# A planned attention and GLU kernel: the third score tile's PSUM banks go to transposes at batch 1's first score tile, and batch 1 counts 35 tiles behind

## The chip, the core and the metric

The kernel runs on one core of a Trainium2 chip. The metric is the device time of one execution in microseconds (us); lower is better. The core has a matrix engine (PE, with its weight loads shown apart as PEld), a vector engine (DVE), a scalar engine (ACT), a GpSimd engine (POOL) and a queue engine that here issues the data transfers (SP). PE writes its results to PSUM, which has 8 banks of 2 KB a partition.

## The reference

```
scores = scale * (q @ k^T)                      # 8 batches, 8 heads, 576 tokens, 64 wide
scores = where(scores >= rowmax(scores) - tau, scores, -1e9)
attn   = softmax(scores);  out = attn @ v
x      = out as 4608 tokens x 512
y      = (sigmoid(x @ w_gate) * (x @ w_val)) @ w_out        # 512 -> 1536 -> 512
```

All of it is float32 in and out; the kernel computes the larger products from high and low parts.

## The kernel before

**Two phases that overlap.** Attention runs over 32 visits, one for each batch and pair of heads. A visit has 9 score tiles of 128 x 576: four for each head and one for the leftover rows of both. For each tile PE computes the scores (s), DVE takes the row maximum (L668) and the threshold (L677), ACT the exponential (L682), DVE the mask and the sum (L685). Then PE transposes the probabilities (tp, and lk for the last keys), ACT copies them out of PSUM (pt, pl, L718), and PE multiplies them with the values (av), which ACT copies to the visit's output xf. The visits of batch 0 use plain scores (L653), the others scores of split operands (L661). The gated unit takes the tokens in 9 blocks of 512. Blocks 0 to 2 are computed directly: m (L863) from x and the weights, then o (L906). Blocks 3 to 8 go in three pairs by a scheme of seven products (qa, qb, qc from L1105, then ra, rb, rc), whose inputs are sums of the two blocks' tokens (L1018, L1010, L1013). Attention's results for them pass through DRAM: xp is written, and read back as xb. The scheme also needs sums of weights, which POOL makes from weights that the first blocks stream (L957, L969, `sums`).

**Conversion.** The weights are split into high and low parts by 36 conversions on POOL (L483, L514), ACT (L487, L508) and DVE (L490, L496), during batch 0's attention. `CONV_IN` and `CONV_OUT` give their keys (first key and step).

**What sets the order.** A planner written in the kernel, `Plan`, does. Each operation is registered with an engine, a cost, a key and its buffers. `run` simulates the engines: an idle engine takes, of the operations whose inputs are done, the one with the lowest key for which `room` finds buffers. After another engine's work it counts a delay, `LAG`, by the engine that waits. The operations are then emitted in that order, so the costs, lags and keys decide what stands where, though the chip runs at its own times. Attention's keys count score tiles: batch 0's visits have keys 0 to 35, and from batch 1 on `SHIFT` is added. The first gated unit's products have key 1e6 and up, so PE takes them where no attention operation is ready; `held_by` keeps attention from running far ahead of them. Ops on `IN_TURN` tags take their buffers in the order of registration.

**PSUM.** Score tiles take two banks each, {0,1}, {2,3} and {4,5}; transposes, av and products take one of {6}, {7} (`homes`). When the first product (key 1e6) is ordered, `started` sets `active["moe"]`: score tiles then have two places, and {4} and {5} go to the single banks. `cap` limits how many single banks each class holds: before that, 3 for attention ("att"); after it, 2 for attention and 2 for products ("moe"). There are only two single banks until then. When the last attention copy is ordered, products may have all four.

Lines that the prediction names: L668, L677, L685 and L682 a score tile's work; L718 ScalarE's copies out of PSUM; L580 and L583 the split of k and q; L756 the normalising of probabilities where it is not done late; L815 the low part of x. A conversion's wa is made by L483 and L496, wb by L487 and L490, ws by L508 and L514.

Of the kernel before, what the change touches and what calls it, by code (L numbers as in the profile page):

```python
# [43 lines left out]
class Plan:  # L44

    IN_TURN = ("x", "xf", "kn", "qn", "vn", "k2", "q2", "kd", "qd", "vs", "p", "pt", "pl", "ptc")

    def __init__(self, pools, slots):  # L50
        self.pools, self.slots = pools, slots
# [92 lines left out]
    def run(self):  # L144
# [3 lines left out]
        events, now, n, dma = [], 0.0, 0, 0.0  # L148
# [6 lines left out]
        while True:  # L155
            moved = True
            while moved:
                moved = False
                for e in engines:
                    if not free[e]:  # L160
                        continue
                    skipped, got = [], None
                    while ready[e]:
                        x = heapq.heappop(ready[e])
                        if self.room(x[2]):
                            got = x[2]
                            break
                        skipped.append(x)
                    for x in skipped:
                        heapq.heappush(ready[e], x)  # L170
                    if got is None:
                        continue
                    moved = True
                    order.append(got)
                    self.started(got)
                    if got.next is not None:
                        got.next.n_deps -= 1
                        if not got.next.n_deps:
                            n += 1
                            heapq.heappush(events, (now, n, "ready", got.next))  # L180
                    free[e] = False
                    if e == "SP":
                        end = now + 0.5
                        dma = max(now + 1.5, dma) + got.cost
                        done = dma + 3.0
                    else:
                        end = done = now + got.cost
                    n += 1
                    heapq.heappush(events, (end, n, "free", e))
                    n += 1  # L190
                    heapq.heappush(events, (done, n, "done", got))
# [3 lines left out]
            while events and events[0][0] <= now + 1e-9:  # L195
                _, _, kind, x = heapq.heappop(events)
# [4 lines left out]
                else:  # L201
# [6 lines left out]
                    for s in x.succ:  # L208
                        lag = 0.0 if s.eng == x.eng else LAG[s.eng]
# [18 lines left out]
    "w": 9, "t2": 6,  # L228
}
LEAD = 8  # L230
CONV_IN, CONV_OUT = (24, 3), (56, 3)


EARLY = 16
# [29 lines left out]

OWN = 24

SHIFT = 50


def LO_DVE(j, out):  # L270
# [2 lines left out]

DVE_LO_IN, DVE_LO_OUT = (), ()

LAG = {"PE": 1.0, "DVE": 0.3, "ACT": 0.08, "POOL": 0.3, "SP": 0.08}

WARM = 16

# [3 lines left out]
    return hp != 3  # L283

FIRST_PAIRS = 4
KD_COST = 1.2

TWOS = ((3, 4), (5, 6), (7, 8))

SUMS_IN, SUMS_OUT, SUM_KEY = {1: (0,), 2: (1,)}, {0: (0,), 1: (1,)}, 300  # L290

AWAY = 2
AHEAD_TWO = 8
# [17 lines left out]
def mm(n):  # L311
    return 0.014 + 0.000418 * n
# [3 lines left out]
def kernel(  # L316
# [25 lines left out]
    nc = tc.nc  # L342
# [12 lines left out]
    HALF = S // 2  # L355
# [32 lines left out]
    ps_more = ahead.enter_context(tc.tile_pool(name="ps_more", bufs=1, space=PSUM))  # L388
# [6 lines left out]
    pools = {t: (sb, n) for t, n in SLOTS.items()}  # L395
    pools["s"], pools["b"] = (ps, 3), (ps, 4)
    slots = {t: n for t, (_, n) in pools.items()}
    active = {"att": 1, "moe": 0}

    class Both(Plan):  # L400
        def cap(self, tag, cls):
            if tag == "s" and active["moe"]:
                return 2 if cls is None else None
            if tag != "b":
                return None
            if cls == "conv":
                return 1
            if cls == "att":
                return 2 if active["moe"] else 3
            return 2 if active["att"] else 4  # L410

        def homes(self, tag):
            if tag == "s":
# [11 lines left out]
            return ps  # L425

        def started(self, o):
            if o.key == 1e6:
                active["moe"] = 1
            if o is last_att[0]:  # L430
                active["att"] = 0

    last_att, more = [None], [ps_more]
    plan = Both(pools, slots)
    op, buf = plan.op, plan.buf

# [92 lines left out]
    class Visit:  # L529
# [32 lines left out]
        def split_scores(self, key, n):  # L562
            b, hp = self.b, self.hp

            kn = buf("kn", [P, SK], F32, f"kn{n}")
            op("SP", 1.2, key - 6, lambda: nc.sync.dma_start(out=kn.ap, in_=k[b, hp]), writes=[kn])


            c0, c1 = self.c0, self.c1 + (2 * SL if self.with_left else 0)
            W, WM = c1 - c0, self.c1 - self.c0  # L570
            qn = buf("qn", [P, W], F32, f"qn{n}")
            op("SP", 1.2, key - 6, lambda: nc.sync.dma_start(out=qn.ap, in_=q[b, hp, :, c0:c1]), writes=[qn])


            k2 = self.k2 = buf("k2", [P, 2, SK + P], F32R, f"k2{n}")
            op("ACT", 0.73, key, lambda: nc.scalar.copy(k2.ap[:, 0, :SK], kn.ap), reads=[kn], writes=[(k2, 0)])
            q2 = self.q2 = buf("q2", [P, 2, W], F32R, f"q2{n}")
            op("ACT", act(W), key, lambda: nc.scalar.activation(q2.ap[:, 0], qn.ap, AF.Copy, scale=scale_t[:, 0:1]),
               reads=[qn], writes=[(q2, 0)])
# [44 lines left out]
    def tile_steps(vis, g, i, key):  # L624
# [5 lines left out]
        s = buf("s", [P, 2, SM], F32, f"s{n}")  # L630
# [32 lines left out]
                        start=m == 0, stop=m == len(steps) - 1,  # L663
                    )

        op("PE", 0.8 if vis.plain_s else len(steps) * 2 * mm(HALF), key, plain_scores if vis.plain_s else scores, reads=reads, writes=[s], also=[g.p], after=held_by(vis))
        st = buf("st", [P, 2], F32, f"st{n}")
        op("DVE", 0.76, key, lambda: nc.vector.tensor_reduce(  # L668
            out=st.ap[:, 0:1], in_=sv(), axis=AX.XY, op=ALU.max, negate=True
# [20 lines left out]
    def late_normalise(vis, key):  # L690
# [13 lines left out]
        for h in range(2):  # L704
# [6 lines left out]
                out=rb.ap[rows, SM:], in_=rd.t[2 * NJ : n, h * SL : (h + 1) * SL].to_broadcast([D, SL])  # L711
            ), reads=[rd], writes=[(rb, (h, 1))])
        op("POOL", 1.5, key, lambda: nc.gpsimd.tensor_tensor(out=vis.xf.ap, in0=vis.xf.ap, in1=rb.ap, op=ALU.mult),
           reads=[rb], writes=[vis.xf], lag=2.0)

    def copy(e, n, key, dst, src, part):
        if e == "ACT":
# [3 lines left out]
    def held_by(vis):  # L721
        n = RATE * (4 * vis.b + vis.hp - 4) - SLACK
        return [unit_ends[n]] if RATE and 0 <= n < len(unit_ends) else []
# [663 lines left out]
```

## Time and profile before

| | |
|---|---|
| median of 3 executions | 1342.62 us (1341.48 to 1343.39) |
| profiled execution | 1342.29 us |
| its span, first to last instruction | 1340.2 us |
| granted PE clock, mean | 0.999 |
| first product of the gated unit starts | 98.13 us |
| last attention product ends | 806.4 us |

The 2.1 us between the profiled execution's own time and its span lie outside the recorded instructions. In rows of a timeline the first number is the start in us, the second the length; the brackets hold how long the engine had been idle and whose work ended that. A row of a group gives, after the bar, its busy time and the mean length of one in ns, then idle time ahead of it. In rows of windows the columns after the length are the busy times of PE, PEld, DVE, ACT and POOL with their counts, the granted PE clock, the busy share of the DMA engines, and GB/s.

### The profile page before, as it was taken

To read this page: it belongs to the slowest core of one execution; us is meant where nothing else is said; L and a number is where in the kernel's file an instruction comes from. 1 tells how busy PE (TensorE), PEld (TensorE's weight loads), DVE (VectorE), ACT (ScalarE), POOL (GpSimd) and SP (SyncE) were. 2 spreads that over 40 slices of the span, in tenths; PEclk is the share of its full clock that TensorE was granted. 3 is DMA by queue.
4 is the path that set the end of the run, shared out by engine and by line. 5 is a ranking of instruction groups with operands and counts; after the bars stand their busy time and mean duration, and the time that the engine had idled before them with its cause. 6 is when DMAs were issued, how large, how long until landed. Compare 5 with 4: busy or idle time off the path is not lost.

```text
span 1340.2 us, 23378 instructions
## 1 busy us (share of the span) xinstructions
PE 1314.8 (98%) x8292; PEld 1077.3 (80%) x8292; DVE 944.4 (70%) x1868; ACT 727.8 (54%) x1339; POOL 492.7 (37%) x474
## 2 busy tenths in 40 slices
PE   8889999999999999999999999999999999999998
PEld 5558887888888888888888888888888888888887
DVE  7888888777787776776777763556955569554594
ACT  8887777667767766666666652223522235322242
POOL 3576867724455363456464441110001010001100
PEclk9999999999999999999999999999999999999999
DMA  8889998999798888998988957656686566756563
GB/s 298 240 260 311 321 259 263 269 260 288 198 254 259 239 241 244 260 293 230 264 246 259 236 190 267 221 191 207 211 286 196 189 204 206 247 178 204 190 217 117
DMA packets 148115, 318.72 MB, mean 238 GB/s; under 512 B 28192, under 2 KB 56096, under 8 KB 148000
## 3 DMA queue, kind: packets, MB, share of 16 engines
q1 hardware_dynamic: 147856, 317.24, 78.3%
q8 instruction: 66, 1.08, 0.3%
q14 instruction: 49, 0.40, 0.1%
q10 hardware_dynamic: 144, 0.00, 0.0%
HBM read 211.16 MB, written 54.64 MB: 198 GB/s over the span
## 4 chain that ended last, share of the span: by engine, by line
PE 91%; DMA 4%; ACT 2%; POOL 1%; DVE 1%; issue 1%; SPq 0%; DVEq 0%; POOLq 0%; ACTq 0%
PE m L863 13%; PE qb L1105 11%; PE av L803 11%; PE s L661 8%; PE tp L767 8%; PE qc L1105 7%; PE qa L1105 7%; PE o L906 7%; PE rb L1170 5%; PE rc L1170 4%; PE ra L1170 4%; PE s_l L661 1%; PE tp_l L767 1%; PE s L653 1%; PE lk L780 1%
## 5 line engine op out<-in xcount | busy, mean ns | idle before, releaser
L668 DVE TENSOR_REDUCE st<-s 128x1 f32<-128x576 f32 x256 | 192.4, 753 | 83.2 <-PE s L661 76.0
L685 DVE SCALAR_TENSOR_TENSOR p<-s,st,p 128x576 f32<-128x576 f32 x256 | 206.5, 813 | 44.7 <-ACT p L682 39.4
L682 ACT ACTIVATE p<-s,st 128x576 f32<-128x576 f32 x256 | 191.1, 751 | 35.1 <-DVE st L668 34.4
L718 ACT COPY pt<-tp 128x512 f32<-128x512 f32 x256 | 149.4, 588 | 83.1 <-PE tp L767 79.1
L1018 POOL TENSOR_TENSOR gA<-gA 128x512 f32<-128x512 f32 x18 | 24.1, 1341 | 409.5 <-DVE gA L1084 409.5
L661 PE MATMUL s<-kd,qd 128*128 128x288 f32 x896 | 163.2, 306 | 2.6 <-DVE p_l L685 1.9
L863 PE MATMUL m<-x,wi 128*128 128x512 f32 x576 | 164.9, 405 | 0.0
L767 PE MATMUL tp<-ident,p 128*128 128x128 f32 x1024 | 155.4, 276 | 8.2 <-ACT pt L718 4.1
L767 PEld LDWEIGHTS tp<-ident,p 128*128 128x128 f32 x1024 | 119.8, 140 | 40.4 <-ACT pt L718 5.6
L661 PEld LDWEIGHTS s<-kd,qd 128*128 128x128 f32 x896 | 134.5, 189 | 13.4 <-DVE p_l L685 2.6
L803 PE MATMUL av<-pt,vs 128*64 128x256 f32 x1024 | 124.6, 385 | 0.8 <-ACT pt L718 0.8
L906 PE MATMUL o<-g,wo 128*128 128x512 f32 x432 | 120.4, 404 | 0.0
L1105 PE MATMUL qa<-xs_p,wa 128*128 128x512 f32 x432 | 109.4, 389 | 0.0
L1042 DVE TENSOR_TENSOR qu<-qb,qp 128x512 f32<-128x512 f32 x72 | 49.8, 692 | 82.5 <-PE qb L1105 71.2
L863 PEld LDWEIGHTS m<-x,wi 128*128 128x128 f32 x576 | 98.0, 189 | 12.0
L803 PEld LDWEIGHTS av<-pt,vs 128*64 128x64 f32 x1024 | 67.9, 136 | 48.5 <-issue 9.5
L1105 PEld LDWEIGHTS qa<-xs_p,wa 128*128 128x128 f32 x432 | 81.1, 188 | 16.8
L906 PEld LDWEIGHTS o<-g,wo 128*128 128x128 f32 x432 | 74.7, 189 | 10.0
L863 PE MATMUL m<-x,ws 128*128 128x512 f32 x288 | 78.5, 404 | 1.5 <-ACT pt L718 1.5
L887 POOL TENSOR_TENSOR g<-th,g 128x512 fp32r<-128x512 f32 x36 | 46.7, 1296 | 58.0 <-ACT g L885 57.8
L756 POOL TENSOR_SCALAR p<-p,zero_t,sm 128x576 f32<-128x576 f32 x64 | 56.5, 892 | 31.1 <-DVE sm L754 19.3
L1010 ACT CAST gs_p<-gA 128x512 fp32r<-128x512 f32 x54 | 32.8, 620 | 61.4 <-DVE gA L1084 23.0
(145 smaller groups left out, 2542.1 us busy)
## 6 DMA issues: line engine op xcount, KB each, us to landing
kd<-k SPq DMA_DIRECT2D x112, 320.0 KB
wi<-wid SPq DMA_DIRECT2D x48, 512.0 KB
wo<-wod SPq DMA_DIRECT2D x36, 512.0 KB
wa<-wid SPq DMA_DIRECT2D x36, 512.0 KB
ws<-sid SPq DMA_DIRECT2D x36, 512.0 KB
wt<-sid SPq DMA_DIRECT2D x36, 512.0 KB
wo_p<-sod SPq DMA_DIRECT2D x36, 512.0 KB
qd<-q SPq DMA_DIRECT2D x112, 128.0 KB
```

Source lines behind the costliest of these rows:

```text
L661: nc.tensor.matmul(s.ap[:, c, :HALF], st(), mv(slice(kc + c * HALF, kc + (c + 1) * HALF)), start=m == 0, stop=m == len(steps) - 1,)
L668: op("DVE", 0.76, key, lambda: nc.vector.tensor_reduce(out=st.ap[:, 0:1], in_=sv(), axis=AX.XY, op=ALU.max, negate=True), reads=[s], write ...
L682: op("ACT", 0.74, key, lambda: nc.scalar.activation(p(), sv(), AF.Exp, bias=st.ap[:, 0:1], scale=1.0), reads=[s, (st, 0)], writes=[(g.p, i)])
L685: op("DVE", 0.9, key, lambda: nc.vector.scalar_tensor_tensor(out=p(), in0=sv(), scalar=st.ap[:, 1:2], in1=p(), op0=ALU.is_ge, op1=ALU.mult ...
L718: return op("ACT", act(n), key, lambda: nc.scalar.copy(dst(), src.ap), reads=[src], writes=[part])
L756: op("POOL", 0.9, key, lambda i=i: nc.gpsimd.tensor_scalar(out=p.ap[:, i * S : (i + 1) * S], in0=p.ap[:, i * S : (i + 1) * S], scalar1=zer ...
L767: nc.tensor.matmul(tp.ap[:, c, :], self.p.ap[:, o + c * P : o + (c + 1) * P], ident, is_transpose=True, start=c == 0, stop=c == NJ - 1, sk ...
L803: nc.tensor.matmul(av.ap[h * D : (h + 1) * D, a:z], vis.vs.ap[:, j, h], m(h), start=i == 0, stop=i == len(ms) - 1, skip_group_check=True,)
L863: nc.tensor.matmul(m.ap, wv[:, a, c * P : (c + 1) * P], xs[c].ap[:, z, c0:c1], start=e == 0, stop=e == 11,)
L906: nc.tensor.matmul(acc.ap, wv[:, f, a], g[fg * ND + f].ap[:, z], start=(fg, f, a, z) == (0, 0, 0, 0), stop=(fg, f, a, z) == (NFG - 1, ND - ...
L1105: nc.tensor.matmul(acc.ap, wv[:, y, (2 * h + c) * P : (2 * h + c + 1) * P], xt[prod][c].get()[:, z], start=e == 0 and prod in FIRST, stop= ...
L1170: nc.tensor.matmul(acc.ap, w.ap[:, e, c, y], gt[prod][2 * g + c].get()[:, z], start=m == 0 and g == 0 and prod in FIRST, stop=m == 5 and g ...
```

## The change

A score tile, batch 1's first (visit 1, 0, tile 0), becomes a second event, `switch`, that sets `active["moe"]`. From there score tiles have two places instead of three, and banks 4 and 5 serve as single banks. Attention holds at most two single banks at any time, and products one until the first of them is ordered (a new flag, "mm"), then two. `SHIFT` goes from 50 to 35, the keys of w_out's conversions from 56 on to 50 on, the weight sums' key from 300 to 120. `LAG` changes for DVE and ACT, the planned cost of a kd load is `KD_COST`, and kn and qn are loaded with keys 8 ahead instead of 6. Two literals get names (`MU_LAG`, `DONE`) with the same values, and two more tags take their buffers in turn.

```diff
-    IN_TURN = ("x", ..., "p", "pt", "pl", "ptc")
+    IN_TURN = ("x", ..., "p", "pt", "pl", "ptc", "pc", "plc")
...
-CONV_IN, CONV_OUT = (24, 3), (56, 3)
+CONV_IN, CONV_OUT = (24,3), (50,3)
-SHIFT = 50
+SHIFT = 35
-LAG = {"PE": 1.0, "DVE": 0.3, "ACT": 0.08, "POOL": 0.3, "SP": 0.08}
+LAG = {"PE":1.0,"DVE":0.2,"ACT":0.3,"POOL":0.3,"SP":.08}
-KD_COST = 1.2
+SWITCH, ATT_BANKS = (1,0,0), 2
+KD_COST = 1.5
+PRE = 8
+MU_LAG = 2.0
+DONE = 3.0
-SUMS_IN, SUMS_OUT, SUM_KEY = {1: (0,), 2: (1,)}, {0: (0,), 1: (1,)}, 300
+SUMS_IN, SUMS_OUT, SUM_KEY = {1: (0,), 2: (1,)}, {0: (0,), 1: (1,)}, 120
...
             if cls == "att":
-                return 2 if active["moe"] else 3
-            return 2 if active["att"] else 4
+                return ATT_BANKS
+            return 1 + active["mm"] if active["att"] else 4
...
         def started(self, o):
+            if o.key == 1e6 or o is switch[0]:
+                active["moe"] = 1
             if o.key == 1e6:
-                active["moe"] = 1
+                active["mm"] = 1
...
-            op("SP", 1.2, key - 6, lambda: nc.sync.dma_start(out=kn.ap, in_=k[b, hp]), writes=[kn])
+            op("SP", 1.2, key - PRE, lambda: nc.sync.dma_start(out=kn.ap, in_=k[b, hp]), writes=[kn])
...
+        if (vis.b, vis.hp, int(key - vis.first)) == SWITCH:
+            switch[0] = scored
```

The lines of the changed kernel's body are 7 to 9 higher in number. In the rows that follow, a name's digits give batch, pair of heads, head and tile, and the last number is the buffer's.

On PE, the last groups ahead of the first product (m, the last row), before:

```order
L661 MATMUL s1_0_021_1326<-kd1_0_0_603,qd1_0_0_842 128x288 x4
L767 MATMUL tp1_0_000_1338<-ident_71,p1_0_00_1250 128x128 x4
L661 MATMUL s1_0_100_1345<-kd1_0_1_851,qd1_0_1_977 128x288 x4
L767 MATMUL tp1_0_001_1357<-ident_71,p1_0_00_1250 128x128 x4
L780 MATMUL lk1_0_00_1366<-ident_71,p1_0_00_1250 128x128
L767 MATMUL tp1_0_l40_1375<-ident_71,p1_0_l4_1220 128x128 x4
L780 MATMUL lk1_0_l4_1387<-ident_71,p1_0_l4_1220 128x128
L661 MATMUL s1_0_101_1391<-kd1_0_1_851,qd1_0_1_977 128x288 x4
L767 MATMUL tp1_0_020_1407<-ident_71,p1_0_02_1362 128x128 x4
L863 MATMUL m0_0_0_0_1417<-x0_0_655,ws0_0_504 128x512 x3
```

And after:

```order
L668 MATMUL s1_0_020_1352<-kd1_0_0_607,qd1_0_0_856 128x288 x4
L776 MATMUL tp1_0_001_1361<-ident_71,p1_0_00_1259 128x128 x4
L789 MATMUL lk1_0_00_1370<-ident_71,p1_0_00_1259 128x128
L668 MATMUL s1_0_021_1372<-kd1_0_0_607,qd1_0_0_856 128x288 x4
L776 MATMUL tp1_0_l40_1386<-ident_71,p1_0_l4_1339 128x128 x4
L789 MATMUL lk1_0_l4_1407<-ident_71,p1_0_l4_1339 128x128
L872 MATMUL m0_0_0_0_1417<-x0_0_656,ws0_0_509 128x512 x3
```

The two score tiles of head 1 (s1_0_100, s1_0_101) and the transpose tp1_0_020 now stand behind the first product.

On POOL, from the last probabilities of pair 3 (p0_3_12) to the last input of the first product (x0_3), before:

```order
L756 TENSOR_SCALAR p0_3_12_1145<-p0_3_12_1145,zero_t_76,sm0_3_12_1183 128x576 x2
L483 TENSOR_SCALAR wa1_2_1243<-wr1_2_1119,zero_t_76 128x512
L514 TENSOR_TENSOR ws4_0_1237<-wa4_0_896,ws4_0_1237 128x512
L580 TENSOR_TENSOR k21_1_1195<-kn1_1_489,k21_1_1195 128x640
L514 TENSOR_TENSOR ws4_1_1273<-wa4_1_915,ws4_1_1273 128x512
L483 TENSOR_SCALAR wa6_0_1317<-wr6_0_1227,zero_t_76 128x512
L815 TENSOR_TENSOR x0_3_1336<-xf0_3_1241,x0_3_1336 128x512
```

And after:

```order
L765 TENSOR_SCALAR p0_3_12_1138<-p0_3_12_1138,zero_t_76,sm0_3_12_1187 128x576 x2
L490 TENSOR_SCALAR wa5_0_1233<-wr5_0_1063,zero_t_76 128x512
L521 TENSOR_TENSOR ws4_1_1230<-wa4_1_927,ws4_1_1230 128x512
L490 TENSOR_SCALAR wa2_2_1262<-wr2_2_1080,zero_t_76 128x512
L490 TENSOR_SCALAR wa5_1_1272<-wr5_1_1119,zero_t_76 128x512
L490 TENSOR_SCALAR wa3_2_1289<-wr3_2_1152,zero_t_76 128x512
L521 TENSOR_TENSOR ws1_2_1270<-wa1_2_1029,ws1_2_1270 128x4x128
L587 TENSOR_TENSOR k21_1_1218<-kn1_1_488,k21_1_1218 128x640
L490 TENSOR_SCALAR wa6_0_1382<-wr6_0_1268,zero_t_76 128x512
L824 TENSOR_TENSOR x0_3_1367<-xf0_3_1287,x0_3_1367 128x512
```

Three more wa of the conversions stand in that stretch, and as many ws as before. The last rows of attention on SP, from the write of its last result (xp from xf7_3) to the load that takes that buffer over (xb0_3_1), before:

```order
L1267 DMA xp2_3_151<-xf7_3_10540 256x1x256
L1278 DMA xp2_3_151<-xf7_3_10540 256x1x32
L841 DMA wo2_3_2_10610<-wod2_130 128x1024
L841 DMA wa20_0_0_10614<-wid0_0_104 128x1024
L841 DMA ws20_0_0_10618<-sid0_0_0_156 128x1024
L841 DMA wt20_0_0_10622<-sid0_0_1_157 128x1024
L1093 DMA wd20_0_0_10626<-wid2_0_108 128x2x256
L841 DMA wa20_0_1_10632<-wid0_1_105 128x1024
L1200 DMA xb0_3_1_10640<-xp0_3_143 128x512
```

And after:

```order
L1276 DMA xp2_3_151<-xf7_3_10580 256x1x256
L1287 DMA xp2_3_151<-xf7_3_10580 256x1x32
L850 DMA ws20_0_1_10645<-sid0_1_0_158 128x1024
L933 DMA out_0_dram<-ot2_2_10641 128x512
L850 DMA wt20_0_1_10661<-sid0_1_1_159 128x1024
L1209 DMA xb0_3_1_10676<-xp0_3_143 128x512
```

All six weight loads now stand ahead of the attention's last writes; between those and xb stand two later weight loads and an output.

More of the change, by code (lines that the diff above doesn't have):

```diff
@@ L44 @@
 class Plan:
-    IN_TURN = ("x", "xf", "kn", "qn", "vn", "k2", "q2", "kd", "qd", "vs", "p", "pt", "pl", "ptc")
+    IN_TURN = ("x", "xf", "kn", "qn", "vn", "k2", "q2", "kd", "qd", "vs", "p", "pt", "pl", "ptc", "pc", "plc")
     def __init__(self, pools, slots):
@@ L184, in run @@
                         dma = max(now + 1.5, dma) + got.cost
-                        done = dma + 3.0
+                        done = dma + DONE
                     else:
@@ L397 @@
     slots = {t: n for t, (_, n) in pools.items()}
-    active = {"att": 1, "moe": 0}
+    active = {"att": 1, "moe": 0, "mm": 0}
     class Both(Plan):
@@ L427, in started @@
         def started(self, o):
+            if o.key == 1e6 or o is switch[0]:
+                active["moe"] = 1
             if o.key == 1e6:
-                active["moe"] = 1
+                active["mm"] = 1
             if o is last_att[0]:
                 active["att"] = 0
-    last_att, more = [None], [ps_more]
+    last_att, switch, more = [None], [None], [ps_more]
     plan = Both(pools, slots)
@@ L571, in split_scores @@
             qn = buf("qn", [P, W], F32, f"qn{n}")
-            op("SP", 1.2, key - 6, lambda: nc.sync.dma_start(out=qn.ap, in_=q[b, hp, :, c0:c1]), writes=[qn])
+            op("SP", 1.2, key - PRE, lambda: nc.sync.dma_start(out=qn.ap, in_=q[b, hp, :, c0:c1]), writes=[qn])
             k2 = self.k2 = buf("k2", [P, 2, SK + P], F32R, f"k2{n}")
@@ L664, in scores @@
                     )
-        op("PE", 0.8 if vis.plain_s else len(steps) * 2 * mm(HALF), key, plain_scores if vis.plain_s else scores, reads=reads, writes=[s], also=[g.p], after=held_by(vis))
+        scored = op("PE", 0.8 if vis.plain_s else len(steps) * 2 * mm(HALF), key, plain_scores if vis.plain_s else scores, reads=reads, writes=[s], also=[g.p], after=held_by(vis))
+        if (vis.b, vis.hp, int(key - vis.first)) == SWITCH:
+            switch[0] = scored
         st = buf("st", [P, 2], F32, f"st{n}")
@@ L713, in late_normalise @@
         op("POOL", 1.5, key, lambda: nc.gpsimd.tensor_tensor(out=vis.xf.ap, in0=vis.xf.ap, in1=rb.ap, op=ALU.mult),
-           reads=[rb], writes=[vis.xf], lag=2.0)
+           reads=[rb], writes=[vis.xf], lag=MU_LAG)
     def copy(e, n, key, dst, src, part):
```

## The prediction

> **What bounds the kernel now.** I read the page's totals first, then its slices, then three windows, then the stretch in which PE loses most.
>
> ```profile
> PE 1314.8 (98%) x8292; PEld 1077.3 (80%) x8292; DVE 944.4 (70%) x1868; ACT 727.8 (54%) x1339; POOL 492.7 (37%) x474
> ...
> PE   8889999999999999999999999999999999999998
> PEld 5558887888888888888888888888888888888887
> ...
> PE 91%; DMA 4%; ACT 2%; POOL 1%; DVE 1%; issue 1%; SPq 0%; DVEq 0%; POOLq 0%; ACTq 0%
> ```
> PE is the bound: it is busy for 98% of the span and carries 91% of the chain that ended last. Both programs issue the same matmuls, so the change can only win PE idle time, or add some. Only the first three slices (0 to 100 us) are below 9. The windows put sizes on them:
>
> ```profile
> 0.00:98.00 98.00, 82.07 (x660) 53.24 (x660) 82.44 (x174) 81.48 (x155) 57.55 (x87) 1.00 0.82 264
> 80.00:98.00 18.00, 14.04 (x122) 10.10 (x120) 17.31 (x35) 15.56 (x31) 14.42 (x15) 1.00 0.83 255
> 98.00:800.00 702.00, 696.58 (x5233) 580.61 (x5233) 530.50 (x1198) 478.42 (x897) 381.71 (x347) 1.00 0.90 257
> 800.00:1336.00 536.00, 536.00 (x2401) 443.43 (x2399) 330.80 (x496) 167.88 (x289) 53.46 (x40) 1.00 0.64 209
> ```
> The columns after the length are PE, PEld, DVE, ACT and POOL. Up to 98 us, when the first MoE product starts, PE is idle for 98 - 82.07 = 15.9 us. Afterwards the idle time is 5.4 us in 702, and then none. So there are three places to examine: the last stretch before the first product, a few stalls in the middle, and the handover at the end of attention, where nothing is lost now but something could be.
>
> **The change part by part.** *Banks for transposes.* PE in the stretch before the first product (start, length, group, idle before it and who ended it), with the last input of that product:
>
> ```profile
> 86.63 0.63 PE L767 MATMUL tp<-ident,p 128*128 128x128 f32 x4 [0.77 <-ACT pt L718]
> ...
> 87.72 0.80 PE L661 MATMUL s<-kd,qd 128*128 128x288 f32 x4 [0.35 <-DVE p L685]
> ...
> 94.61 0.66 PE L767 MATMUL tp_l<-ident,p_l 128*128 128x128 f32 x4 [0.57 <-ACT pt L718]
> ...
> 96.80 0.65 PE L767 MATMUL tp<-ident,p 128*128 128x128 f32 x4 [0.65 <-ACT pl_l L718]
> 98.13 0.50 PE L863 MATMUL m<-x,ws 128*128 128x512 f32 x1 [0.68 <-ACT pt L718]
> ...
> 92.62 1.28 POOL L815 TENSOR_TENSOR x<-xf,x 128x512 fp32r<-128x512 f32 x1 [1.53 <-ACT x L813]
> ```
> Four groups wait until ScalarE has copied an earlier transpose out of its bank: 0.77 + 0.57 + 0.65 + 0.68 = 2.67 us. The product's last input was ready at 92.62 + 1.28 = 93.90, 4.2 us before it started. In the changed order these transposes can use banks 4 and 5 too, so this wait should go. What takes its place is the loss of the third score tile, hence waits such as the 0.35 us on p, since a score bank is free only when VectorE has read it.
>
> The changed order puts two score tiles and one transpose group behind the first product instead of ahead of it. The rows of the stretch from 80 to 98 us (count, busy and mean):
>
> ```profile
> L661 PEld LDWEIGHTS s<-kd,qd 128*128 128x128 f32 x24 | 3.4, 191 | 1.3 <-DVE p L685 1.0 <-DVE st L668 0.2
> L767 PEld LDWEIGHTS tp<-ident,p 128*128 128x128 f32 x20 | 2.1, 140 | 2.9 <-POOL wa L483 1.0 <-ACT pl_l L718 0.9 <-POOL p L756 0.6
> L668 DVE TENSOR_REDUCE st<-s 128x1 f32<-128x576 f32 x6 | 4.5, 751 | 0.2 <-PE s L661 0.2
> L685 DVE SCALAR_TENSOR_TENSOR p<-s,st,p 128x576 f32<-128x576 f32 x5 | 4.0, 813 | 1.6 <-POOL st L677 1.6
> L490 DVE SCALAR_TENSOR_TENSOR wb<-wb,wa 128x512 int32<-128x512 int32 x5 | 3.5, 691 | 0.0
> L496 DVE SCALAR_TENSOR_TENSOR wa<-wr,wb 128x512 int32<-128x512 int32 x5 | 3.4, 687 | 0.2
> L677 DVE TENSOR_SCALAR st<-st,ntau_t 128x1 f32<-128x1 f32 x5 | 1.1, 212 | 0.1
> L483 POOL TENSOR_SCALAR wa<-wr,zero_t 128x512 f32<-128x512 f32 x5 | 4.8, 959 | 1.2 <-DMA wr<-in_moe_w_out_dram 1.2
> L514 POOL TENSOR_TENSOR ws<-wa,ws 128x512 fp32r<-128x512 f32 x4 | 5.1, 1282 | 0.0
> ```
> PE defers 2 x 4 x 3.4/24 = 1.13 us of scores and 4 x 2.1/20 = 0.42 us of transposes, 1.55 us. Starting the product 1.55 us earlier therefore wins nothing; only what is beyond that counts. VectorE is relieved of 2 x 0.751 + 2 x 0.813 + 0.212 = 3.34 us and gets two L490 and one L496 more, 2.07 us: 1.27 us less. POOL, between the last probabilities of pair 3 and x of pair 3, gets three more wa and the same number of ws: 3 x 0.959 = 2.88 us. So x would be ready at 93.90 + 2.88 = 96.8 if POOL comes to that stretch as late as before, and near 93.9 if it comes that much earlier. The product then starts 98.13 - 96.8 = 1.3 to 98.13 - 93.9 = 4.2 us earlier, which less 1.55 gives between 0.2 lost and 2.7 won. But VectorE is 17.31 us busy of 18 here. If it paces this stretch, the product comes 1.27 us earlier, less than the 1.55 deferred, and 0.3 is lost. Ends: +0.3 and -2.7. I take -1.2, their middle, since the rows show both a product that waits past its input and a nearly full VectorE.
>
> How much was there to win at all? By the PE row, this window has 18 - 14.04 = 3.96 us idle. [...]
>
> *Stalls in the middle.* These are the five large ones, with the instruction behind the second, its usual length, the POOL sum ahead of the fifth, and the granted clock after the second (the number ahead of the last two columns):
>
> ```profile
> 122.80 1.42 PE L863 MATMUL m<-x,ws 128*128 128x512 f32 x5 [0.80 <-ACT pt L718]
> ...
> 219.60 0.80 PE L661 MATMUL s<-kd,qd 128*128 128x288 f32 x4 [1.91 <-DVE p_l L685]
> ...
> 509.78 0.44 PE L803 MATMUL av<-pt,vs 128*64 128x256 f32 x2 [0.37 <-ACT pt L718]
> ...
> 609.33 0.66 PE L767 MATMUL tp<-ident,p 128*128 128x128 f32 x4 [1.26 <-ACT pt_l L718]
> ...
> 705.64 0.66 PE L767 MATMUL tp<-ident,p 128*128 128x128 f32 x4 [0.84 <-POOL p L756]
> ...
> 212.30 5.18 DVE L583 SCALAR_TENSOR_TENSOR q<-qn,scale_t,q 128x640 fp32r<-128x640 f32 x1
> ...
> L583 DVE SCALAR_TENSOR_TENSOR q<-qn,scale_t,q 128x640 fp32r<-128x640 f32 x1 | 1.5, 1457 | 0.0
> ...
> 702.80 1.97 POOL L969 TENSOR_TENSOR s<-s 128x512 fp32r<-128x512 f32 x1
> ...
> 220.00:222.00 2.00, 2.00 (x12) 1.71 (x10) 1.64 (x4) 0.33 (x1) 2.00 (x2) 0.60 0.96 205
> 222.00:224.00 2.00, 2.00 (x8) 1.80 (x8) 0.75 (x2) 1.92 (x4) 1.47 (x3) 0.54 0.91 199
> ```
> They add up to 5.18 us, and the clock at 0.60 and 0.54 of full for 2 us each costs 0.80 + 0.92 = 1.72 more: 6.9 us. The order decides whether they come again: attention's keys from batch 1 on now lie 15 lower against those of the conversions, and the planner assumes longer hand-overs to ScalarE. Of 56 first products of probabilities with values, 24 stand less than 2 us of PE work behind their last transpose before the change, and 16 after it (counted in the orders, with durations of the trace). Taking a third off the waits on pt gives (0.80 + 0.37 + 1.26)/3 = 0.8. The event at 219.6 comes from one VectorE instruction of 5.18 us, which takes 1.46 elsewhere (the row of L583 is of the stretch from 80 to 98 us); as the instructions around it change, I give it an even chance to come again: half of 1.91 + 1.72 is 1.8. Together -2.6, ends 0 and -6.9.
>
> On that clock: the Trainium skill ("TensorE: Matmul & The Clock Gate", "What's actually happening") has the clock halved after some 3.4 us of idling. By that rule the 1.91 us gap would have kept full speed and half the event would be 1.0, a sum smaller by 0.9. The row disagrees, and it decides.
>
> *Handover.* After the last attention product, PE has o matmuls until qa; the late rows are these:
>
> ```profile
> 806.16 0.29 PE L803 MATMUL av<-pl_l,vs 128*64 128x64 f32 x4
> 806.38 15.73 PE L906 MATMUL o<-g,wo 128*128 128x512 f32 x68
> 821.95 1.52 PE L1105 MATMUL qa<-xs_p,wa 128*128 128x512 f32 x6
> ...
> 827.39 1.52 PE L1105 MATMUL qb<-xs_p,ws 128*128 128x512 f32 x6
> ...
> 820.33 3.78 POOL L1018 TENSOR_TENSOR xb<-xb,xb 128x512 f32<-128x512 f32 x3 [21.49 <-DMA xb<-xp]
> 824.64 1.29 DVE L1013 TENSOR_TENSOR xs_p<-xb,xs_p 128x512 fp32r<-128x512 f32 x2 [19.55 <-ACT xs_p L1010]
> ```
> The last av frees the xf buffer once its write has landed; the last xb is loaded into it, POOL adds, and the first qb reads the split. Its data are ready about 824.64 + 1.29/2 = 825.3, 18.9 us after 806.38; qb needs them at 827.39. The cover was 15.57 + 5.44 = 21.0 us; in the changed order 42 o matmuls are left, 42 x 15.57/68 = 9.6, so 15.0 us. Were the chain as long as before, qb would stall for 3.9 us. But SP issues six weight loads (2.75 MB) between those writes and the xb load before, and two loads and one output (1.25 MB) after; at the middle's 257 GB/s that saves 1.5/0.257 = 5.8 us and leaves 13.1, with 1.9 to spare. I take 0; ends 0 and +3.9.
>
> *The rest.* SUM_KEY lets POOL's weight sums go ahead of attention's work from tile 120 on: the stall at 705.64 is of that kind (POOL did a sum of L969 from 702.80 to 704.77). I take 0, with ends -0.8 (it goes) and +2.5 (three more like it). PRE and KD_COST only move kn, qn and kd issues on SP; no PE wait on them is among those above, so 0. If that cover fails, one 320 KB load at 257 GB/s costs 1.2 us. CONV_OUT is in the POOL and VectorE counts above. The larger ScalarE LAG has no price of its own. The IN_TURN tags have one buffer each, so nothing waits, and MU_LAG and DONE keep their values: 0.
>
> Sum: -1.2 - 2.6 + 0 + 0 = -3.8. The profiled execution took 1342.29 (span 1340.2 and 2.1 around it): 1338.5. It lies 0.33 below the median of 1342.62, which I leave inside the range. About 0.2%, 2.7 us, is what a measurement can tell.
>
> **The rivals.** (B) VectorE paces the start and the middle's stalls come back elsewhere: +0.3 and 0, so 1342.6. For it: 17.31 us of 18, and that every reordering makes new tight places. Against it: those four waits name ScalarE's bank copies.
> (C) The handover stalls. If SP's load of xb is held up by the wait for a weight buffer ahead of it, and ScalarE does two further copies of 0.6 before the split, the chain stays at 18.9 + 1.2 and qb waits 5.1 us: 1347.4 with nothing else won, 1343.6 with my other terms. It decides the sign from a chain of 15.0 + 3.8 = 18.8 us, about its present length. Against it: fewer bytes ahead of xb.
> (D) Sums on POOL delay attention: each costs 0.84 as at 705.64; eight of them give +6.7 less 3.8, so 1345.2. Five undo the gain. Against it: POOL is 381.71 us busy in 702.
> (E) None of the large stalls recurs: -1.2 - 6.9, so 1334.2. For it: the longest comes from an instruction that took 5.18 us only there.
> (F) The switch is early on paper only, since products do not start earlier: the changed order already shows it in force, so this merges into B.
>
> **How the numbers follow.** Forecast (1336 to 1340): 0.42. E: 0.12. B (1340 to 1345): 0.27. C: 0.10. D: 0.09. Faster by over 0.2% are the forecast and E, 0.54; within it B, and a mild part of C and D, 0.29; slower 0.17. The range leaves out the far ends of E, C and D: 1332.5 to 1345.2. The forecast's own is 1336 to 1340.
>
> **What would show it.** The first product should start at 94 to 96 us, with no wait on pt or pl_l ahead of the transposes in the 10 us before it; if it starts past 97, B holds. The window from 98 to 800 should hold about 3 us of PE idle, not 5.4; a VectorE instruction of 5 us again keeps 3.6. The first qb should follow the qa and qc without a gap: a wait there by ScalarE or VectorE on xs_p is C. Waits of tp on POOL p behind L969's successors are D. I am wrong if the start is paced by VectorE or if the handover's chain is over 15 us.

## The result: faster by 0.8%, more than twice the forecast gain

The changed kernel took 1333.63 us (median of 6 runs, 1331.9 to 1336.95), the kernel before 1343.43 us beside it (6 runs, 1341.48 to 1347.93). The ratio on record is 0.9916 with a 95% interval of 0.9892 to 0.9941; the two medians alone give 0.9927, inside it. The forecast was 1338.5 us in a range of 1332.5 to 1345.2: the time lies inside, the direction is right, and the gain is 9.8 us by the medians (8.1 us between the two profiled executions, 1342.29 and 1334.22) where 3.8 were forecast.

The page's totals of the changed kernel, its chain, and the three windows that answer to those of before:

```profile
span 1332.4 us, 23397 instructions
...
PE 1312.8 (99%) x8292; PEld 1079.2 (81%) x8292; DVE 935.3 (70%) x1858; ACT 732.0 (55%) x1349; POOL 493.6 (37%) x474
...
PE 95%; ACT 2%; DVE 1%; issue 1%; DMA 0%; POOL 0%; POOLq 0%; DVEq 0%; ACTq 0%
```
```profile
0.00:98.00 98.00, 83.97 (x656) 55.37 (x656) 82.62 (x175) 82.80 (x158) 60.76 (x90) 0.97 0.85 277
80.00:98.00 18.00, 15.60 (x135) 11.85 (x133) 16.46 (x34) 16.81 (x34) 15.73 (x16) 1.00 0.81 263
98.00:800.00 702.00, 701.48 (x5283) 588.05 (x5282) 520.60 (x1189) 483.04 (x908) 379.03 (x344) 1.00 0.90 259
```
The first 98 us gained 1.9 us of PE busy time. The middle is where the time went: PE is now idle for 702 - 701.48 = 0.5 us of it, against 5.4 before.

Idle time by the row understates what is lost, since a PE that runs slowly still counts as busy. So in what follows **loss** means: for each matmul, the time until the next one starts, less what a matmul of its size takes in undisturbed stretches (227 ns with 512 columns, 130 with 288, 109 for a 128-column transpose, and so on), summed over a stretch. The work so counted is 1264.6 us in every kernel here, and the losses of two kernels differ as their spans do: 71.2 and 62.9 us, a difference of 8.3, against spans that differ by 7.8. (The rest lies behind PE's last matmul.)

| loss in us | to 100 us | 100 to 180 | 180 to 780 | 780 to 880 | sum | o matmuls behind the last av | splits of q, sum |
|---|---|---|---|---|---|---|---|
| before | 32.3 | 4.0 | 33.6 | 1.3 | 71.2 | 68 | 40.7 |
| changed | 31.9 | 3.2 | 25.9 | 2.0 | 62.9 | 42 | 32.4 |

So of 8.3 us, 0.4 came from the start, 0.8 and 7.7 from the middle, and 0.7 was given back at the handover.

### The profile page after: what moved, and what is told of

It reads as the page before. It is cut to its first block, busy times and chain, and to the rows that moved or that the text cites. A ratio compares the mean times of both kernels' runs of the same rounds, so it can differ in the third digit from the quotient of the medians.

```text
span 1332.4 us, 23397 instructions
## 1 busy us (share of the span) xinstructions
PE 1312.8 (99%) x8292; PEld 1079.2 (81%) x8292; DVE 935.3 (70%) x1858; ACT 732.0 (55%) x1349; POOL 493.6 (37%) x474
## 4 chain that ended last, share of the span: by engine, by line
PE 95%; ACT 2%; DVE 1%; issue 1%; DMA 0%; POOL 0%; POOLq 0%; DVEq 0%; ACTq 0%
PE m L872 15%; PE av L812 11%; PE qb L1114 11%; PE s L668 9%; PE tp L776 8%; PE o L915 7%; PE qa L1114 7%; PE qc L1114 7%; PE rb L1179 6%; PE rc L1179 4%; PE ra L1179 4%; PE s_l L668 2%; PE s L660 1%; PE lk L789 1%; PE tp_l L776 1%
## 5 line engine op out<-in xcount | busy, mean ns | idle before, releaser
L694 DVE SCALAR_TENSOR_TENSOR p<-s,st,p 128x576 f32<-128x576 f32 x256 | 206.3, 812 | 32.6 <-ACT p L691 30.3
L691 ACT ACTIVATE p<-s,st 128x576 f32<-128x576 f32 x256 | 191.9, 751 | 37.2 <-DVE st L677 36.5
L1027 POOL TENSOR_TENSOR gA<-gA 128x512 f32<-128x512 f32 x18 | 24.1, 1342 | 407.4 <-DVE gA L1093 407.4
L776 PEld LDWEIGHTS tp<-ident,p 128*128 128x128 f32 x1024 | 120.9, 141 | 34.6 <-ACT pt L727 4.8
L1019 ACT CAST gs_p<-gA 128x512 fp32r<-128x512 f32 x54 | 32.9, 622 | 61.1 <-DVE gA L1093 23.0
```

The source lines that it names most:

```text
L691: op("ACT", 0.74, key, lambda: nc.scalar.activation(p(), sv(), AF.Exp, bias=st.ap[:, 0:1], scale=1.0), reads=[s, (st, 0)], writes=[(g.p, i)])
L694: op("DVE", 0.9, key, lambda: nc.vector.scalar_tensor_tensor(out=p(), in0=sv(), scalar=st.ap[:, 1:2], in1=p(), op0=ALU.is_ge, op1=ALU.mult ...
L776: nc.tensor.matmul(tp.ap[:, c, :], self.p.ap[:, o + c * P : o + (c + 1) * P], ident, is_transpose=True, start=c == 0, stop=c == NJ - 1, sk ...
```

## The experiments

Each run is one kernel with one profile; ratios are to the kernel before on the same chip. The loss is that of one execution, and executions differ: on one chip, 22 of the kernel before lay between 1338.42 and 1352.53 us. In the two that have a trace, its loss differs by 1.1, 2.1 and 1.4 us in the first three stretches of the table, so differences of that size between two single traces tell little.

**1. The two kernels again.** No edit.

> A second profile of the kernel before. Theory 1 (the large stalls belong to the order of instructions): the stalls at about 121, 609 and 705 us stand at the same places with about the same lengths (0.8, 1.3, 0.8 us). Theory 2 (they are accidents of one execution): at most one of them is there again. For the VectorE instruction of 5.18 us at 212 us, theory 1 expects it again with 3 to 5 us and a PE gap of about 2 us behind it; theory 2 expects 0.95 to 1.5 us and no gap, so a span about 3.6 us shorter, near 1336.5 us.

> A second profile of the changed kernel. In the first one the granted clock fell to 0.50 and 0.69 from 58 to 62 us behind a stretch with PE idle. If the order causes it, it is there again and the span is near 1332.4 us; if it is an accident, it is gone and the span is 1 to 2 us shorter. The small gap behind the first qb products (0.9 us of loss from 820 to 860 us) should be there again in both cases, since it follows from the handover.

Before: 1347.22 us. The gaps at m (now at 123.9), at av on pt (513.8) and at tp on pt_l (613.5) are there again, the one on POOL's p at 705 is not, and there are six others, the wait behind the split among them. The long split of q is there again, but two visits earlier, and PE waits behind it again. The execution's rows around it (POOL's work, VectorE's split, and the PE group that waited):

```profile
158.78 1.29 POOL L514 TENSOR_TENSOR ws<-wa,ws 128x512 fp32r<-128x512 f32 x1
...
159.61 3.91 DVE L583 SCALAR_TENSOR_TENSOR q<-qn,scale_t,q 128x640 fp32r<-128x640 f32 x1
160.02 1.56 POOL L580 TENSOR_TENSOR k<-kn,k 128x640 fp32r<-128x640 f32 x1
...
161.55 1.29 POOL L514 TENSOR_TENSOR ws<-wa,ws 128x512 fp32r<-128x512 f32 x1
162.97 1.22 POOL L483 TENSOR_SCALAR wa<-wr,zero_t 128x512 f32<-128x512 f32 x1
...
164.43 0.79 PE L661 MATMUL s<-kd,qd 128*128 128x288 f32 x4 [1.43 <-DVE p_l L685]
```
The split runs from 159.61 to 163.52, through three POOL instructions that follow each other without a gap, and ends 0.68 us after the third of them, which ends at 162.84. So neither theory held as written: the event is no accident of one execution, and it doesn't belong to one place either. Loss from 180 to 780: 35.0 us.

Changed: 1334.32 us, loss 63.1 us, from 180 to 780 us 26.2, and from 820 to 860 again 0.9. The first execution's clock of 0.50 and 0.69 at 58 to 62 us is not there again (1.00 over that stretch), so it belonged to that execution; but neither the span (1332.5 us) nor the loss up to 100 us (31.8) is shorter without it, so the loss expected of it isn't seen. In both executions the longest wait of PE in the middle is 0.3 us; in the two of the kernel before it is 1.9 and 1.6 us.

**2. The bank policy alone, and everything else alone.** To the kernel before, the switch and the caps:

```diff
-                return 2 if active["moe"] else 3
-            return 2 if active["att"] else 4
+                return 2
+            return 1 + active["mm"] if active["att"] else 4
...
-            if o.key == 1e6:
+            if o.key == 1e6 or o is switch[0]:
```

> The kernel before with the bank policy alone (the switch at batch 1's first score tile, attention at two single banks, products at one until the first of them). Theory S (the banks carry the gain): 8 to 10 us faster than before, and the first product at 95 to 97 us. Theory O (the gain is the sum of stalls in the middle that the whole new order happens to avoid, the banks only win the start): 1 to 3 us faster, start of the first product at 95 to 97 us, with large stalls at other places in the middle.

1351.92 us, ratio 1.0059 (1.0040 to 1.0079): slower, which neither theory expected. The first product starts at 98.22, the loss up to 100 us is 33.9, so the start wins nothing. The middle loses 5.7 and 34.2 us, as before, and from 820 to 860 us, with 18 o matmuls behind the last av, 4.7 us are lost where before lost none. The other half, the changed kernel with the old bank policy:

```diff
-SWITCH, ATT_BANKS = (1,0,0), 2
+SWITCH = None
...
-                return ATT_BANKS
-            return 1 + active["mm"] if active["att"] else 4
+                return 2 if active["moe"] else 3
+            return 2 if active["att"] else 4
```

> The changed kernel with the bank policy of before (three score tiles until the first product) and all its other numbers. Theory S: as slow as before, 1342 to 1344 us. Theory O: 1334 to 1338 us, with the waits on pt back ahead of the first product, which starts at 97 to 99 us.

1342.36 us, ratio 0.9981 (0.9964 to 0.9998), where neither theory put it. Its start loses 33.6 us (first product at 99.20, so the banks may win 1.7 us there once the rest is changed, little more than the 1.1 by which two executions of one kernel differ), its middle 4.5 and 27.8, and from 820 to 860 us it loses 5.0. The rows of PE at that place:

```profile
814.05 0.29 PE L812 MATMUL av<-pl_l,vs 128*64 128x64 f32 x4
814.27 4.38 PE L915 MATMUL o<-g,wo 128*128 128x512 f32 x18
...
823.93 0.84 PE L1114 MATMUL qb<-xs_p,ws 128*128 128x512 f32 x3
826.06 0.49 PE L1114 MATMUL qb<-xs_p,ws 128*128 128x512 f32 x1 [1.29 <-ACT xs_p L1019]
827.19 0.73 PE L1114 MATMUL qb<-xs_p,ws 128*128 128x512 f32 x2 [0.63 <-DVE xs_p L1022]
```
Only 18 o matmuls stand between the last attention product and qa, and qb waits for the split of the late tokens. This is the stall of the prediction's rival C, in another order than the one it was forecast for.

**3. One number undone at a time.** Each is the changed kernel with one old value: `LAG`; `KD_COST = 1.2` and `PRE = 6`; `SUM_KEY = 300`; `SHIFT = 50`; `CONV_OUT = (56, 3)`.

> The changed kernel with the LAG numbers of before. Theory P (the middle's gain comes from VectorE's split of q, L583, no longer running beside a busy POOL, and every number that shifts POOL's or VectorE's order can bring it back): the 28 splits of q take 36 to 41 us in all (32.4 in the changed kernel, 40.7 before), and the middle from 100 to 800 us loses 2 to 5 us more than the changed kernel's. Theory L (the lags carry the gain): as slow as before, 1342 us or more. Under both the handover's loss follows the o matmuls left behind the last attention product: none at 68, 0.9 us at 42, 5 us at 18.

> The changed kernel with kn and qn loaded 6 keys ahead and a planned 1.2 for kd. Theory P: kn and qn arriving earlier lets the two splits of q and k start apart; with the old numbers the splits of q take 36 us or more in all, and the time is 1336 to 1340 us. Theory L: no difference, 1333 to 1335 us, splits at 32 to 33 us. The handover again by the o matmuls left.

> The changed kernel with the weight sums at key 300, behind attention's work on POOL. If sums ahead of attention's work made new stalls (rival D of the prediction), this is faster than the changed kernel by 1 us or more. If they moved POOL's work out of VectorE's way, the splits of q take longer than 32.4 us in all and the time is 1335 us or more. If the key matters only at the end, the o matmuls left behind the last attention product change from 42 and only the handover's loss differs.

> The changed kernel with SHIFT at 50. Attention's keys meet the conversions' and the sums' keys later. I expect 1333 to 1336 us, with the first 98 us as in the changed kernel within 0.5 us, and a start of the first product at 95.5 to 97 us. If the shift carried the gain it would be at 1342.

> The changed kernel with w_out's conversions at keys 56 on, as before. PE begins the first seven-product block ahead of the last attention products here, so no o matmul covers the handover: by the rows of the other runs (8.1 us at 0, 11.6 us where qc already came first) I expect 8 to 13 us lost from 800 to 860 us, and 1341 to 1350 us.

| | us | ratio to before | to 100 us | 100 to 180 | 180 to 780 | 780 to 880 | o matmuls left | splits of q |
|---|---|---|---|---|---|---|---|---|
| LAG old | 1350.34 | 1.0035 (1.0014 to 1.0056) | 34.6 | 2.5 | 32.0 | 9.8 | 0 | 36.8 |
| loads old | 1354.12 | 1.0073 (1.0045 to 1.0100) | 34.6 | 2.8 | 30.5 | 15.3 | 0 | 33.8 |
| sums at 300 | 1334.46 | 0.9921 (0.9895 to 0.9947) | 33.3 | 3.0 | 26.0 | 1.3 | 56 | 35.3 |
| SHIFT 50 | 1347.45 | 1.0010 (0.9989 to 1.0031) | 31.1 | 3.1 | 31.2 | 7.8 | 4 | 35.3 |
| conversions at 56 | 1358.41 | 1.0093 (1.0059 to 1.0128) | 35.3 | 7.1 | 26.4 | 20.2 | 0 | 32.9 |

Four of the five edits, undone, cost the whole gain or more, and about half to seven tenths of what they lose is lost at one place, the handover: 7.8 us or more with four o matmuls left or none, 1.3 with 56. In the long middle, too, undoing `SHIFT` or the loads' numbers (31.2 and 30.5 us) costs nearly as much as undoing the lags (32.0). Most expectations missed. The old lags did what both theories expected (splits of 36.8 us, a middle worse by 5.4, over 1342 us), so that run doesn't part them; the old loads did what neither did (splits of 33.8 us, 1354.12 us). shift_50 was expected to cost 2 us at most. conv_56 lost 20 us at the end instead of 8 to 13 (besides 4.5 us of qb, transposes wait 4.1 us on POOL's p there). sum_300 doesn't tell its cases apart by time: splits of q at 35.3 us in all without a stall, so their sum is no measure of the loss, and a start 1.4 us worse against a handover 0.7 better. Rival D, sums that delay attention, is not seen.

**4. The handover's chain cut.** The last token load goes into a buffer that doesn't wait for attention's last write (the gate keeps it from being taken too early):

```diff
-        tags = iter(["qd"] * 3 + ["kn", "qn", "vn"] + ["xf"] * 2)
+        tags = iter(["qd"] * 3 + ["kn", "qn", "vn"] + ["xf", "t2" if k == 0 else "xf"])
...
-                ), reads=[xp_d[k][hp]], writes=[b])
+                ), reads=[xp_d[k][hp]], writes=[b], after=gate if (k, hp, z) == (0, 3, 1) else [])
...
+        if (vis.b, vis.hp) == (7, 3) and key == vis.first:
+            gate.append(scored)
```

> The changed kernel with the bank policy of before, and the last token load ahead of the first seven-product block put into a free buffer of another tag, so that it doesn't wait for attention's last write. If the 5.0 us lost from 820 to 860 us follow from that wait (the handover's chain against 18 o matmuls), they fall to 1 us or less and the time to 1337 to 1339 us. If they come from the weights' loads or from POOL, they stay at 4 us or more and the time at 1341 us or more.

> The changed kernel with the last token load in a free buffer of another tag, as in the run beside it. The handover's 0.9 us should go and nothing else change: 1332 to 1333.5 us, 0.5 to 1 us faster than the changed kernel, which the timing alone may not tell apart; the trace's loss from 820 to 860 us does.

Without the switch, 1338.03 us, ratio 0.9961 (0.9946 to 0.9975), and nothing is lost from 820 to 860 us, still with 18 o matmuls. So the wait for that buffer is the cause of the 5.0 us. PE in the same two stretches, first with the old buffer, then with the free one:

```profile
820.00:860.00 40.00, 37.34 (x156) 29.95 (x155) 23.73 (x33) 12.55 (x21) 8.40 (x6) 0.96 0.66 218
```
```profile
820.00:860.00 40.00, 40.00 (x178) 33.13 (x177) 22.43 (x34) 9.50 (x16) 4.53 (x4) 1.00 0.64 212
```
In the changed kernel the cut takes the 0.9 us away as well, but the time, 1334.38 us, ratio 0.9933 (0.9917 to 0.9949), can't be told from the changed kernel's. No version tried beats it clearly.

**5. VectorE's split of q.** First the low part of q is made by POOL in the kernel before, with the same order; then it is made three times in the changed kernel:

```diff
-            op("DVE", ..., lambda: nc.vector.scalar_tensor_tensor(out=q2.ap[:, 1], in0=qn.ap, ..., in1=f32(q2.ap[:, 0]), ...)
+            op("DVE", ..., lambda: [nc.gpsimd.tensor_scalar(out=qn.ap, in0=qn.ap, ..., scalar2=scale_t[:, 0:1], ...),
+                nc.gpsimd.tensor_tensor(out=q2.ap[:, 1], in0=qn.ap, in1=f32(q2.ap[:, 0]), op=ALU.subtract)], ...)
```

> The kernel before with the low part of q (L583 on VectorE, two SBUF inputs) made on POOL by two instructions; the order of every other instruction stays. POOL gets about 28 x 2.5 = 70 us more, VectorE 40 us less. Theory P (PE's stalls from 100 to 800 us come from VectorE's split of q held up while POOL works): the loss there falls from 37.6 to 32 us or less, and the time to 1338 us or less. Theory K (the order itself is too tight, whoever makes the split): the loss stays at 37 us or more, with waits on POOL in place of those on VectorE.

> The changed kernel with the same split of q written three times in a row by VectorE, the same values each time; the order stays. The 28 splits then take 28 x (2 x 0.88 + 1.16) = 82 us or more in all, as long one by one as the stretched ones of before or longer. Theory P (the changed kernel is free of stalls because its splits are short): it loses as much as before in the middle, 1340 us or more. Theory K (its order has room for late VectorE work): within 2 us of the changed kernel, 1333 to 1336 us.

With the split on POOL: 1350.46 us, ratio 1.0061 (1.0040 to 1.0082), loss from 100 to 780 us 43.6. PE's wait on p_l is gone, but six waits of transposes on POOL's p took its place:

```profile
PE tp L769 <- POOL p L758: 2.9, 6, 1.1
PE tp L769 <- ACT pt_l L720: 2.0, 1, 2.0
```
This run added 28 x (0.88 + 1.56) = 68 us to POOL, so, although the loss and the waits are what theory K expected, it doesn't separate the two theories; it only shows POOL's own work to be close to the path too. With the split made three times, the changed kernel's loss from 100 to 780 us goes from 29.0 to 75.0 us and the time to 1391.92, ratio 1.0360 (1.0341 to 1.0379):

```profile
PE s L668 <- DVE p_l L694: 31.2, 21, 3.0
```
The group is what a longer split delays: 21 score groups wait, in nearly every visit, 1.5 us each. 70.7 us more on VectorE cost 46 us on PE. So theory K falls for this order: it has no room for a VectorE that is late by that much. That fits an order that is free of stalls because nothing makes VectorE late there, but doesn't show it: the dose (3.7 us a visit, in every visit) is far stronger than the one long split of before, so it gives the direction and not the size.

**6. The lags.** The kernel before with the changed `LAG` alone, and with the lags, the loads' numbers and the free buffer of experiment 4:

> The kernel before with the changed LAG alone; 70 o matmuls stand behind the last attention product, so the handover should cost nothing. Theory L (the lags make the order roomy): loss from 100 to 780 us near 30 us, against 29 in the changed kernel and 38 to 41 before, and the time 1334 to 1337 us. Theory J (only the joint order does it): loss 34 us or more, 1338 to 1343 us.

> The kernel before with the changed LAG, the kn and qn loads 8 keys ahead, the planned 1.5 for kd, and the last token load in a free buffer of another tag, since only 10 o matmuls stand behind the last attention product. Theory L, with the loads: splits of q at 33 us or less in all, loss from 100 to 780 us near 30 us, 1334 to 1337 us. Theory J: 34 us or more, 1338 to 1343 us. From 820 to 860 us less than 1 us is lost by either.

| | us | ratio to before | to 100 us | 100 to 180 | 180 to 780 | 780 to 880 | splits of q |
|---|---|---|---|---|---|---|---|
| lags alone | 1344.46 | 0.9996 (0.9975 to 1.0016) | 33.7 | 10.6 | 26.6 | 1.2 | 33.7 |
| lags, loads, free buffer | 1339.24 | 0.9962 (0.9945 to 0.9980) | 33.8 | 4.4 | 27.8 | 2.3 | 35.0 |

By the time, and by the loss from 100 to 780 us that both theories named (37.2 us), theory J holds in the first run. In the second the time is J's, the loss (32.2) lies between the two, and the splits of q miss theory L's 33 us. The places, looked at afterwards, tell more. From 180 to 780 us the lags alone bring nearly the whole gain, 7.0 of 7.7 us, and lose 6.6 again from 100 to 180 us. PE's named waits from 180 to 780 us, before and then with the lags alone:

```profile
PE s L661 <- DVE p_l L685: 1.9, 1, 1.9
PE tp L767 <- ACT pt_l L718: 1.3, 1, 1.3
PE tp L767 <- POOL p L756: 0.8, 1, 0.8
PE av L803 <- ACT pt L718: 0.4, 1, 0.4
```
```profile
PE tp L767 <- ACT pt_l L718: 0.3, 1, 0.3
```
And the windows from 100 to 180 and from 180 to 780 us, lags alone and then before:

```profile
100.00:180.00 80.00, 77.09 (x514) 61.41 (x515) 66.82 (x138) 61.84 (x116) 51.56 (x46) 0.98 0.98 307
180.00:780.00 600.00, 599.58 (x4600) 501.02 (x4599) 439.90 (x1020) 405.35 (x761) 316.11 (x287) 1.00 0.88 250
```
```profile
100.00:180.00 80.00, 79.20 (x542) 65.25 (x541) 66.10 (x138) 61.21 (x118) 54.55 (x47) 1.00 1.00 301
180.00:780.00 600.00, 595.51 (x4562) 497.40 (x4561) 446.09 (x1017) 403.74 (x757) 314.13 (x289) 1.00 0.90 253
```
About 3 of the 10.6 us lie ahead of 108 us and belong to the start, which is late there: the first product comes at 104.08, and just ahead of it PE runs at about half its clock:

```profile
102.00:104.00 2.00, 1.84 (x9) 1.41 (x8) 2.00 (x6) 1.97 (x5) 1.06 (x1) 0.52 0.91 289
```
Read with experiment 3 (the lags undone: 32.0 us from 180 to 780, against 25.9), two opposite edits agree that the lags decide much of the long middle: in the kernel before they are nearly enough, and in the changed kernel they are needed. They are not enough in every order: with the new lags and the old `SHIFT` or the old loads, 31.2 and 30.5 us are lost there. The other numbers also keep the lags' price down elsewhere: 10.6 us from 100 to 180 us with the lags alone, 4.4 with the loads and the free buffer as well, 3.2 with everything; and the handover at 2.0 us instead of 6 to 20.

## Why the prediction was wrong in size

**The start (-1.2).** Between the profiled executions the loss up to 100 us fell by 0.4 us, between the second pair by 1.6 (33.4 to 31.8). The term was about right, and VectorE didn't pace the start (rival B): PE's waits there name ScalarE. Its mechanism was half right: the product came at 96.09 with its input ready at 95.36, and ScalarE's copies still hold up PE, at other rows; one of them, 0.72 us on pl, stands in the last 10 us, where no such wait was expected. PE and the input in the changed kernel:

```profile
81.93 0.63 PE L776 MATMUL tp<-ident,p 128*128 128x128 f32 x4 [0.66 <-ACT pt L727]
...
84.64 0.63 PE L776 MATMUL tp<-ident,p 128*128 128x128 f32 x4 [0.83 <-ACT pl L727]
...
95.61 0.33 PE L789 MATMUL lk_l<-ident,p_l 128*128 128x128 f32 x1 [0.72 <-ACT pl L727]
96.09 1.20 PE L872 MATMUL m<-x,ws 128*128 128x512 f32 x4 [0.15 <-ACT pt_l L727]
...
94.08 1.28 POOL L824 TENSOR_TENSOR x<-xf,x 128x512 fp32r<-128x512 f32 x1
```
The product moved up by 2.04 us, of which the deferred 1.55 wins nothing: 0.5.

**The stalls in the middle (-2.6): the step that failed.** They were worth 8.5 us by loss (37.6 to 29.0 from 100 to 780 us), 11.8 in the second pair (41.1 to 29.3). The places were the right ones; the size came out at a third. Two of its choices were wrong. "Taking a third off the waits on pt" counted how far a product stands behind its transpose on PE; but all five waits went, from 5.2 us to 0.3 in all. And "an even chance to come again" took the 5.18 us split for an oddity of one instruction. It is a collision with POOL that came again in the second execution of before at another place, and in neither of the changed kernel's. The splits' sum points the same way (40.7 and 40.1 us before, 32.4 and 32.6 after), though other orders show that the loss doesn't follow it. Rival E, with no large stall recurring, put 1334.2 us at a chance of 0.12; its mechanism is what happened to the middle. That its time meets the profiled 1334.22 is partly luck: its terms were -1.2, -6.9 and 0, and the losses changed by -0.4, -8.5 and +0.7. The third error is the lag: the prediction named the longer assumed hand-overs to ScalarE among what decides whether the stalls come again, and yet gave the lag "no price of its own". The two new lags, ScalarE's and VectorE's together, cost 6.1 us of the long middle when they were undone, and brought 7.0 when they were put alone into the kernel before. Why they do is open: with the new lags the splits are shorter (33.7 against 40.7 us), and PE may also have other work ahead of its waits; no run parts the two.

**The handover (0, up to +3.9).** +0.7 us. The rows there in the changed kernel:

```profile
803.15 9.82 PE L915 MATMUL o<-g,wo 128*128 128x512 f32 x42
812.81 1.52 PE L1114 MATMUL qa<-xs_p,wa 128*128 128x512 f32 x6
...
818.25 1.53 PE L1114 MATMUL qb<-xs_p,ws 128*128 128x512 f32 x6
...
823.09 1.66 PE L1114 MATMUL qb<-xs_p,wt 128*128 128x512 f32 x6 [0.57 <-DVE qu L1051]
...
818.23 0.69 DVE L1022 TENSOR_TENSOR xs_p<-xb,xs_p 128x512 fp32r<-128x512 f32 x1 [10.95 <-ACT xs_p L1019]
```
The first qb didn't wait; a later one did, for VectorE, which does the late splits in one run. That the handover was close was right, and that 42 o matmuls would just do. The cover was right too: 15.1 us from 803.15 to 818.25, with 15.0 forecast. The chain was not: by the prediction's own way of reading it, it took 818.23 + 0.69 - 803.15 = 15.8 us, against 18.9 before and 13.1 forecast. So fewer bytes ahead of xb saved about 3 us and not 5.8, nothing was to spare instead of 1.9 us, and the prediction's sign of being wrong, a chain over 15 us, came without the stall that it stood for. Orders with the same PE work, but with 18 o matmuls there or fewer and the old buffer, lose 6 to 20 us.

**Banks as the headline.** The edit in the title, by itself, made the kernel slower, and without it the rest of the change gains 0.2%. Each of the other numbers that were undone, but the sums' key, is as necessary to the time; the two tags were not tried by themselves. The gain belongs to the joint order. Of its parts the runs isolate one, the wait at the handover and its cover; the lags in the middle are shown to matter, together with `SHIFT` and the loads, and not by what mechanism.

## What to carry to other kernels

Where a planner writes the order, an edit's effect on the whole time is the sum of several stretches that move against each other; split the span into stretches, and compare edits in each. Two kernels of equal time (before, and the lags alone) differed by 7.0 us in one stretch and by 6.6 the other way in the one ahead of it. A chain that crosses a phase's end is priced by the work that covers it: count that work in the order, and look for the buffer that ties the chain to the phase's last write.

## What the runs showed of the hardware

**VectorE held up by POOL.** The split of q (L583) reads two SBUF operands. Its group from 100 to 800 us before, and in the changed kernel:

```profile
L583 DVE SCALAR_TENSOR_TENSOR q<-qn,scale_t,q 128x640 fp32r<-128x640 f32 x26 | 38.3, 1471 | 8.6 <-ACT q L578 7.4 <-DMA xp<-xf 0.8
```
```profile
L590 DVE SCALAR_TENSOR_TENSOR q<-qn,scale_t,q 128x640 fp32r<-128x640 f32 x26 | 30.5, 1175 | 8.2 <-ACT q L585 7.3 <-DMA xp<-xf 0.5
```
```profile
121.87 0.88 DVE L590 SCALAR_TENSOR_TENSOR q<-qn,scale_t,q 128x640 fp32r<-128x640 f32 x1
```
The single row is one of the changed kernel's with POOL idle: 0.88 us. In the two kernels' traces the splits took up to 2.27 us beside one to three POOL instructions, and 3.91 and 5.18 beside four in a row; other orders had 3.36 beside three (the old lags) and 4.15 beside four (conversions at 56). All four long ones ended 0.68 us after the end of a POOL instruction, the longest after the fourth beside it and the others after the third. L490, the same kind of instruction with 512 columns and one operand in PSUM, took 0.692 us on average with POOL busy all along and 0.695 with POOL idle. The Trainium skill ("SBUF — State Buffer", section "SBUF: two separate sides") says that VectorE with two SBUF inputs and GpSimd share a port pair as an exclusive lock; the traces agree, and show in addition that one VectorE instruction can stay held up through several POOL instructions in a row. The prediction had the row with 5.18 us and didn't see POOL's work beside it.

It goes the other way too. Ahead of the wait at 705.64 us before, POOL made two sums of L969, and a split of q began 0.05 us ahead of the second:

```profile
701.55 3.22 POOL L969 TENSOR_TENSOR s<-s 128x512 fp32r<-128x512 f32 x2
702.75 0.88 DVE L583 SCALAR_TENSOR_TENSOR q<-qn,scale_t,q 128x640 fp32r<-128x640 f32 x1
```
The split took its 0.88 us, and the second sum took 1.97 us where the first took 1.25. So about 0.7 us of the 0.84 us that the prediction put down to a sum standing ahead of attention's work is, by this estimate, the same collision.

**The clock after short gaps.** In the changed kernel without the switch, the clock over 828 to 832 us, behind the gaps of 1.29 and 0.63 us shown above, was 0.60:

```profile
828.00:832.00 4.00, 3.27 (x8) 2.48 (x8) 4.00 (x5) 2.86 (x5) 1.89 (x2) 0.60 0.52 138
```
Those 4 us at 0.60 lose 1.6 us besides the 1.92 us of the gaps, so this stall cost nearly twice its length, as did the one at 219.6 us before (1.91 and 1.72). It is not so behind every such gap. In the kernel before, behind the gap of 1.26 us at 609.33, and in its second execution, behind one of 1.64 us at 513.76, the clock stayed full:

```profile
610.00:612.00 2.00, 2.00 (x11) 1.65 (x11) 1.43 (x3) 1.81 (x4) 1.51 (x3) 1.00 0.95 262
```
```profile
514.00:516.00 2.00, 2.00 (x26) 1.47 (x24) 1.13 (x3) 1.81 (x4) 0.57 (x1) 1.00 1.10 237
```
What sets the two kinds apart, no run here shows.
